# Experts' inner values split straight out of PSUM, size sums on ScalarE, conversion steps placed behind each scale, 4 KB rows for the second matrices

## The chip, the core and the metric

One core of a Trainium2 chip runs the whole program. Five engines take part: TensorE (PE in the rows; its weight loads are PEld), VectorE (DVE), ScalarE (ACT), GpSimd (POOL), and SyncE (SP), which issues nearly all the DMAs. Each engine works through its own list of instructions in order and waits on semaphores for the others. The metric is the device time of one execution in microseconds; lower is better.

## The reference

The program computes three layers one after the other: retention attention, a mixture of experts with a "sticky" choice of expert, and a Fourier mixing layer with a channel network. Only the middle one bears on the change:

```python
for b in range(B):
    for s in range(S):
        e = fresh_e if s == 0 or local_gate[b, s] < 0.5 else prev_e
        h = np.maximum(x[b, s] @ w1[e], 0.0)        # w1[e]: 512 x 1024
        out[b, s] = p[e] * (h @ w2[e])              # w2[e]: 1024 x 512
# last layer: ch = np.maximum(un @ w_ch1, 0.0) @ w_ch2, both matrices given as 64-bit floats
```

There are 2304 tokens and 8 experts. Everything is wanted at about fp32 accuracy.

## The kernel before

**Halves.** TensorE is fed fp16. Every fp32 operand is divided by a power-of-two scale and written as two fp16 tiles, high and low, and a product is the sum of three: high·high, low·high, high·low. For a weight matrix this is done on the chip, per piece of 128 rows x 1024 values (8 pieces per expert: 0 to 3 are the first matrix, 4 to 7 the second, which is loaded with two 2 KB rows per partition):

- `load` (L224): one 512 KB DMA from SP into a buffer of the pool `wst`.
- `absmax`/`size` (L234 on ScalarE by a sum of absolute values, L236 on VectorE by a maximum): the size of the piece. The table `SUMS` puts pieces 0 and 1 on VectorE and 2 to 7 on ScalarE.
- `peak` (L250, L251, L255): VectorE joins four sizes and writes a diagonal, `diag`; `spread` (L260 on TensorE, L261 on VectorE): a matmul of 128x128 with that diagonal brings the largest size to all partitions; `scale` (L266, L269): VectorE makes the scale `ws` and its inverse.
- `split`: `high` (L276, ScalarE, needs `ws`) and `low` (L281, VectorE, needs the high half).

**Conversion.** In the same stage VectorE converts the channel matrices of the last layer, which come as 64-bit floats, in 14 jobs of 128x1024 values: SP loads 1 MB (`conv.load`, L322, tile `raw`, two buffers), `first` is three instructions (L294, L296, L298), `second` two (L303, L306), `store` writes 512 KB (L338), `conv.absmax` takes the size (L234 or L236, alternately).

**An expert** has two steps. In the *hidden* step TensorE makes eight blocks f = 0..7 of the inner values (`products`, L807: 12 matmuls of n columns each, n = 416, 320, 320, 320, 288, 288, 128 for experts 1 to 7). Each block has a PSUM bank of the pool `p1`, which has four. `relu` takes a block away: ScalarE writes max(x, 0) as fp32 to a tile `r` (L818), ScalarE rounds that to the high half (L820), GpSimd subtracts the two for the low half (L822). In the *outputs* step the tokens go in tiles of 128: 24 matmuls per tile (L834, eight chunks of three), then a copy with the factor `fs` on ScalarE (L846) and an indirect DMA from GpSimd (L848). A rest of 64 or 32 tokens is done as 2 or 4 matmuls side by side.

**What sets the order.** The instructions are emitted by hand. `halves(weights, conv, n, slots)` gives the side jobs of step n (even: hidden of expert n/2, odd: its outputs), and the table `SLOTS` (one dictionary for even, one for odd steps) gives each a place between 0 and 8; all jobs that fall into one block or one tile are emitted, in the order of their places, ahead of that block's `relu` or that tile's copy. Step n splits the matrix that step n + 1 reads, sizes that of step n + 2 and loads that of step n + 3. In a hidden step TensorE does block 0, then the `spread` matmul of the expert's own second matrix, then blocks 1 to 7. In an outputs step the `spread` of the next expert's first matrix stands behind the fourth chunk of the first tile. Experts 0 and 1 start by hand (`begin`, `parts`, `first`, `convert`). On SP the token fetch for expert e + 1 (`fetch`, L1003: a transposing DMA, and L1016, L1019 for the indices) stands at the head of the hidden step of expert e. The last expert's rest is done by `Late` in the stage behind.

## Time and profile before

| what | us |
|---|---|
| median of three runs | 809.13 (806.35 to 814.45) |
| the profiled execution | 809.86 |
| its span in the trace | 808.1 |
| TensorE busy in the span | 741.5 (92%) |
| VectorE busy | 604.2 (75%) |
| ScalarE busy | 418.9 (52%) |
| GpSimd busy | 189.6 (23%) |

The page's table in 40 slices (20.2 us each) shows attention in slices 0 to 6, the experts in slices 6 to 17, and the last layer behind. All times below are from the start of the span. A row of a timeline reads: start, duration, engine, line, instruction, tile written <- tiles read, shape, count; in brackets the idle time ahead of it and what ended that.

### The profile page before, as it was taken

The page shows a single profiled execution, that of the slowest core. Times are in us where ns is not written, and L with a number is a line of the kernel's source. Part 1 is how long each engine was busy: PE and PEld are TensorE (multiplying, and loading weights), DVE is VectorE, ACT ScalarE, POOL GpSimd, SP SyncE. Part 2 cuts the span into 40 slices and gives each one's busy share as a digit, 9 for nine tenths or more (in the row PEclk, how much of TensorE's full clock was granted, in tenths as well). Part 3 has the DMA queues.
Part 4 walks back from the last instruction along what each step waited for, and adds up shares of the span by engine and source line. Part 5 has one row for each costly group of instructions (what it writes and reads, how often), then busy time and mean ns, then how long its engine had stood idle before and what let it go on. Part 6 is the DMA issues. An engine that isn't in the chain of part 4 may idle for free. (4 is left out here: it accounts for less than half of the span.)

```text
span 808.1 us, 17327 instructions
## 1 busy us (share of the span) xinstructions
PE 741.5 (92%) x6571; PEld 552.4 (68%) x6571; DVE 604.2 (75%) x1390; ACT 418.9 (52%) x857; POOL 189.6 (23%) x289
## 2 busy tenths in 40 slices
PE   8898898899899898789998999989889999999996
PEld 5687775546556555566644547868778888888885
DVE  3578988877898898857787986978958495737362
ACT  1356654778788787864744643515423361504140
POOL 3566442544355245322100002010010101010101
PEclk9999999999999999999998999999999999999998
DMA  9998349889899889932256357620380016110000
GB/s 294 348 302 312 108 131 306 226 296 374 312 280 322 319 248 310 351 110 91 84 175 236 127 192 204 188 68 2 112 198 2 27 53 171 53 33 21 27 2 27
DMA packets 91932, 142.30 MB, mean 176 GB/s; under 512 B 48116, under 2 KB 49017, under 8 KB 90814
## 3 DMA queue, kind: packets, MB, share of 16 engines
q1 hardware_dynamic: 87246, 126.78, 48.9%
q0 software_dynamic: 4592, 14.31, 4.6%
q8 instruction: 54, 0.88, 0.4%
q14 instruction: 40, 0.33, 0.1%
HBM read 97.55 MB, written 35.12 MB: 164 GB/s over the span
## 5 line engine op out<-in xcount | busy, mean ns | idle before, releaser
L1613 PE MATMUL g<-gxt,wh 128*128 128x256 f16 (+1 forms) x992 | 143.5, 285 | 3.6 <-DMA gxt<-un 3.4
L1927 PEld LDWEIGHTS <-hd 128*128 128x128 f16 x1176 | 114.7, 98 | 26.6 <-issue 6.4
L1613 PEld LDWEIGHTS <-wh 128*128 128x128 f16 x1056 | 103.1, 98 | 29.7 <-issue 8.4
L281 DVE SCALAR_TENSOR_TENSOR wl<-wst,ws,wh 128x1024 f16<-128x1024 f32 (+1 forms) x82 | 102.9, 1288 | 20.4 <-ACT wh L276 20.1
L1787 POOL DMA_INDIRECT out<-u,orow x18 | 19.1, 1064 | 391.2 <-DVE u L1956 293.3
L276 ACT ACTIVATE wh<-wst,ws 128x1024 f16<-128x1024 f32 x80 | 88.8, 1141 | 35.5 <-DVE ws L269 35.5
L807 PE MATMUL ps<-xt,wh 128*128 128x320 f16 (+4 forms) x544 | 81.3, 292 | 6.6 <-DMA xt<-xs 3.6
L807 PEld LDWEIGHTS <-wh 128*128 128x128 f16 x640 | 59.4, 103 | 38.7 <-issue 20.8
L834 PE MATMUL ps<-wh,hid 128*128 128x512 f16 (+2 forms) x528 | 84.2, 302 | 0.5 <-POOL hid L822 0.5
L1927 PE MATMUL g<-wh,hd 128*128 128x256 f16 x448 | 78.3, 273 | 2.9 <-DVE s L1898 1.6
L1613 PE MATMUL g<-gxt,wl 128*128 128x256 f16 (+1 forms) x496 | 80.5, 285 | 0.0
L1898 DVE SCALAR_TENSOR_TENSOR s<-g,r 128x256 f32<-128x256 f32 x168 | 53.1, 370 | 31.3 <-ACT hd L1892 30.5
L834 PEld LDWEIGHTS <-hid 128*128 128x128 f16 (+2 forms) x792 | 46.3, 100 | 42.5 <-issue 2.5
L822 POOL TENSOR_TENSOR hid<-r,hid 128x320 f16<-128x320 f32 (+3 forms) x64 | 64.0, 1011 | 41.4 <-ACT hid L820 40.8
L1956 DVE SCALAR_TENSOR_TENSOR u<-g,ffs,u 128x256 f32<-128x256 f32 (+1 forms) x63 | 34.1, 567 | 49.3 <-PE g L1927 48.7
L1891 ACT ACTIVATE r<-g 128x256 f32<-128x256 f32 x56 | 21.2, 379 | 92.8 <-PE g L1613 86.8
L1927 PE MATMUL g<-e,hd 128*128 128x256 f16 x504 | 61.2, 276 | 5.4 <-DVE u L1956 4.4
L1871 ACT ACTIVATE hd<-s 128x640 f16<-128x640 f32 x56 | 41.3, 737 | 46.8 <-DVE s L1898 46.8
L1927 PE MATMUL g<-wl,hd 128*128 128x256 f16 x224 | 61.1, 273 | 0.0
L1613 PEld LDWEIGHTS <-wl 128*128 128x128 f16 x528 | 51.8, 98 | 11.8 <-issue 1.1
L234 ACT ACTIVATE wh<-wst 128x1024 bf16<-128x1024 f32 x51 | 53.5, 1050 | 9.1 <-DMA wst<-in_moe_w 5.1
L834 PE MATMUL ps<-wl,hid 128*128 128x512 f16 (+2 forms) x264 | 56.3, 302 | 0.0
(303 smaller groups left out, 1352.3 us busy)
## 6 DMA issues: line engine op xcount, KB each, us to landing
wst<-in_moe_w SPq DMA_DIRECT2D x64, 512.0 KB
raw<-in_ch SPq DMA_DIRECT2D x14, 1024.0 KB
qk<-in_qkv SPq DMA_DIRECT2D x18, 512.0 KB
vk<-in_qkv SPq DMA_DIRECT2D x16, 512.0 KB
pair<-ch SPq DMA_DIRECT2D x32, 256.0 KB
ch<-d SPq DMA_DIRECT2D x14, 512.0 KB
...
```

Of the source, the lines that this page charges most:

```text
L234: self.nc.scalar.activation(out=x, in_=t, func=ACTF.Abs, accum_out=self.am[:, j : j + 1])
L276: self.nc.scalar.activation(out=self.dst[0][:, j, :], in_=self.pieces[j], func=ACTF.Copy, scale=self.by(j))
L281: self.nc.vector.scalar_tensor_tensor(out=l[:, j, c], in0=self.pieces[j][:, c], scalar=self.by(j), in1=h[:, j, c], op0=ALU.mult, op1=ALU.s ...
L807: nc.tensor.matmul(out=ps, lhsT=m[:, k, 128 * f : 128 * f + 128], rhs=xt[:, x + k, :], start=(k == 0 and i == 0), stop=(k == 3 and i == 2),)
L822: e.tensor_tensor(out=l[:, f, :], in0=r, in1=h[:, f, :], op=ALU.subtract)
L834: nc.tensor.matmul(out=ps[r * j : r * j + r, 0:d], lhsT=hid[x][:, f, 128 * t : 128 * t + r], rhs=m[:, 4 + f // 2, c : c + d], start=(f == ...
L1613: nc.tensor.matmul(out=ps, lhsT=m[:, k + 4 * (f // 8), 128 * (f % 8) : 128 * (f % 8) + 128], rhs=xt[x][:, k, :], start=(k == 0 and i == 0) ...
L1871: nc.scalar.activation(out=hd[:, 0, 2:7], in_=s, func=ACTF.Copy, scale=C2 / 2)
L1891: nc.scalar.activation(out=r, in_=p[:, 1:3], func=ACTF.Relu)
L1898: V.scalar_tensor_tensor(out=d, in0=x, scalar=0.0, in1=y, op0=ALU.max, op1=op)
L1927: nc.tensor.matmul(out=ps, lhsT=hid[k][:, y, x, :], rhs=E[w][m][k], start=(k == 0 and m == y == 0), stop=(k == 7 and y == 1),)
L1956: V.scalar_tensor_tensor(out=y, in0=p, scalar=fs[:, c : c + 1], in1=y, op0=ALU.mult, op1=ALU.add)
```

## The change

- **relu.** ScalarE writes the high half of a block directly from PSUM (one instruction in place of two), and VectorE makes the low half from the same PSUM bank: max(x, 0) - high, in place of GpSimd's subtraction. The factor `C1` goes into the scales (`W1_TOP`, `X_TOP`), so that no factor is applied on the way.
- **Sizes.** All sizes of weights and of conversion jobs are taken on ScalarE (`sums=S0` for all).
- **Order.** New `SLOTS`; conversion jobs run one step further ahead than before; in step 2 (hidden of expert 1) jobs 2 and 3 both stand at place 0. Loads of both matrices of expert e + 2 stand in the outputs step of expert e (the second ones at `ahead`), `fetch` stands behind the first splits, the factors of the outputs go among VectorE's side jobs (`factors`). Expert 2's pieces 4 to 7 are loaded in `sizes`.
- **Second matrix.** A partition gets two neighbouring rows (one run of 4 KB) in place of two rows 128 apart (2 x 2 KB). So that the inner values meet the right rows, the split of the first matrix reads every second column (`turned`), and `outputs` takes the chunks as 0, 4, 1, 5, 2, 6, 3, 7.

The diff, cut to its core:

```diff
+    def turned(self, j, c=slice(0, 1024)):
+        h, l, x = self.dst[0][:, j, c], self.dst[1][:, j, c], self.pieces[j]
+        if self.one or j > 3:
+            return h, l, x[:, c]
+        by = lambda w: w.rearrange("k (a q) -> k a q", q=512)
+        return by(h), by(l), x.rearrange("k (q a) -> k a q", a=2)[:, c.start // 512 : c.stop // 512, :]
...
     def high(self, j):
-        self.nc.scalar.activation(out=self.dst[0][:, j, :], in_=self.pieces[j], func=ACTF.Copy, scale=self.by(j))
+        h, _, x = self.turned(j)
+        self.nc.scalar.activation(out=h, in_=x, func=ACTF.Copy, scale=self.by(j))
...
-def relu(nc, e, ps, r, hid, f):
-    nc.scalar.activation(out=r, in_=ps, func=ACTF.Relu, scale=C1)
+def relu(nc, ps, hid, f, r=None):
     h, l = hid
-    nc.scalar.copy(out=h[:, f, :], in_=r)
+    if r is not None:
+        nc.scalar.activation(out=r, in_=ps, func=ACTF.Relu)
+        ps = r
+    nc.scalar.activation(out=h[:, f, :], in_=ps, func=ACTF.Relu)
     yield
-    e.tensor_tensor(out=l[:, f, :], in0=r, in1=h[:, f, :], op=ALU.subtract)
+    nc.vector.scalar_tensor_tensor(out=l[:, f, :], in0=ps, scalar=0.0, in1=h[:, f, :], op0=ALU.max, op1=ALU.subtract)
...
-    for f in range(8):
+    for s, f in enumerate((0, 4, 1, 5, 2, 6, 3, 7)):
...
 SLOTS = [
     dict(
-        split=(0, 0, 1, 2),
-        load=(1.5, 2.5, 2.5, 4.5),
-        size=(3.6, 4.6, 5.6, 5.7),
-        first=1.4,
+        own=-1,
+        second=0,
+        split=(0.1, 1.1, 2.1, 3.1),
+        raw=1.2,
+        store=1.3,
+        fetch=1.4,
+        size=(2.6, 3.6, 4.6, 5.6),
         peak=6.3,
-        bound=6.4,
     ),
     dict(
-        split=(0.5, 1.5, 2.5, 3.5),
+        own=-1,
+        first=(0, 4.2),
+        factors=0.2,
+        split=(0.5, 0.6, 1.5, 2.7),
+        second=2.8,
         load=(2, 3, 4, 5),
         size=(3.1, 4.1, 4.6, 5.2),
-        rest=0.2,
-        early=0.25,
-        first=0.3,
-        second=3.6,
-        store=6.9,
-        raw=0.5,
-        other=2.0,
-        bound=5.9,
+        raw=5.5,
+        store=5.6,
         peak=7.3,
+        ahead=(7.4, 7.5, 7.6, 7.7),
     ),
 ]
...
+    if n == 2:
+        at(S["second"], conv.first, 2)
+        ends(2)
+        at(S["peak"], conv.absmax, 2)
+        at(S["second"], conv.first, 3)
+    if n % 2 and n + 1 < DONE:
+        at(S["first"][0], conv.first, n + 1)
+    ends(n + 1)
+    if n % 2 and n + 2 < DONE:
+        at(S["first"][1], conv.first, n + 2)
...
-            r = wk.tile([128, CAP], FP32, tag="r", name="r", bufs=3)[:, 0:n]
-            for _ in relu(nc, nc.gpsimd, ps, r, hid, f):
+            for _ in relu(nc, ps, hid, f):
                 pass
...
-                    A["moe_w2"][e, 256 * j : 256 * j + 256, :].rearrange("o (a p) d -> p (o a) d", p=128)
+                    A["moe_w2"][e, 256 * j : 256 * j + 256, :].rearrange("o (p a) d -> (o p) a d", a=2).rearrange("p a d -> p (a d)")
```

`ends(j)` places `second`, `store` and the load of job j + 2.

**VectorE in the hidden step of expert 1**, from the scale of the expert's second matrix on (`wl` is a weight's low half, `d` and `raw` a conversion job, `am` a size, `hid` the low half of a block of inner values). Before:

```order
L269 RECIPROCAL ws<-wi 128x1
L281 SCALAR_TENSOR_TENSOR wl_78<-wst,ws,wh_77 128x1024 x3
L294 TENSOR_SCALAR d<-raw 128x1024
L296 TENSOR_SCALAR d<-d 128x1024
L298 TENSOR_SCALAR d<-d 128x1024
L281 SCALAR_TENSOR_TENSOR wl_78<-wst,ws,wh_77 128x1024
L236 TENSOR_REDUCE am<-wst 128x1 x2
```

And now, up to the low half of block 1:

```order
L302 TENSOR_SCALAR d<-raw 128x1024
L304 TENSOR_SCALAR d<-d 128x1024
L306 TENSOR_SCALAR d<-d 128x1024
L311 SCALAR_TENSOR_TENSOR d<-raw,d 128x1024
L314 SCALAR_TENSOR_TENSOR d<-raw,d 128x1024
L302 TENSOR_SCALAR d<-raw 128x1024
L304 TENSOR_SCALAR d<-d 128x1024
L306 TENSOR_SCALAR d<-d 128x1024
L311 SCALAR_TENSOR_TENSOR d<-raw,d 128x1024
L314 SCALAR_TENSOR_TENSOR d<-raw,d 128x1024
L291 SCALAR_TENSOR_TENSOR wl_78<-wst,ws,wh_77 128x1024
L833 SCALAR_TENSOR_TENSOR hid<-ps_2360,hid 128x416
```

Two whole conversion jobs, 2 and 3, have moved ahead of the first low halves, and the low half of block 0 of the inner values stands behind all of them.

**TensorE at the start of block 4 of expert 1** with the semaphores that are waited for (`ps_2458` and `ps_2454` are block 3, `ps_2477` and `ps_2472` block 4, the fifth block, which takes the bank of block 0 again). Before:

```order
L807 MATMUL ps_2458<-xt,wh_77 128x416
L807 LDWEIGHTS wh_77
L807 MATMUL ps_2477<-xt,wh_77 128x416 [waits Activation_49]
L807 LDWEIGHTS wh_77
L807 MATMUL ps_2477<-xt,wh_77 128x416
```

And now:

```order
L815 MATMUL ps_2454<-xt,wh_77 128x416
L815 LDWEIGHTS wh_77
L815 MATMUL ps_2472<-xt,wh_77 128x416 [waits DVE_49]
L815 LDWEIGHTS wh_77
L815 MATMUL ps_2472<-xt,wh_77 128x416
```

The bank was given back by ScalarE and is now given back by VectorE.

**VectorE in the outputs step of expert 2**, from the middle of the step (`wg`, the answer to the spread matmul) to the next diagonal. Before:

```order
L261 TENSOR_REDUCE wg<-ps_3057 128x1
...
L303 SCALAR_TENSOR_TENSOR d<-raw,d 128x1024
L306 SCALAR_TENSOR_TENSOR d<-raw,d 128x1024
L294 TENSOR_SCALAR d<-raw 128x1024
L296 TENSOR_SCALAR d<-d 128x1024
L298 TENSOR_SCALAR d<-d 128x1024
L281 SCALAR_TENSOR_TENSOR wl_78<-wst,ws,wh_77 128x1024 x4
L303 SCALAR_TENSOR_TENSOR d<-raw,d 128x1024
L306 SCALAR_TENSOR_TENSOR d<-raw,d 128x1024
...
L255 TENSOR_SCALAR diag<-idn,wm 128x128
```

And now:

```order
L302 TENSOR_SCALAR d<-raw 128x1024
L304 TENSOR_SCALAR d<-d 128x1024
L306 TENSOR_SCALAR d<-d 128x1024
L1069 TENSOR_TENSOR fs<-wi 128x1
L1070 TENSOR_SCALAR fs<-mt,fs 128x3
L1164 TENSOR_SCALAR mt<-mt,side_1982 128x1
L291 SCALAR_TENSOR_TENSOR wl_78<-wst,ws,wh_77 128x1024 x4
L311 SCALAR_TENSOR_TENSOR d<-raw,d 128x1024
L314 SCALAR_TENSOR_TENSOR d<-raw,d 128x1024
L302 TENSOR_SCALAR d<-raw 128x1024
L304 TENSOR_SCALAR d<-d 128x1024
L306 TENSOR_SCALAR d<-d 128x1024
```

One `second` has left the stretch (it stands in the hidden step, right behind the scale there), one `first` and the three small instructions for the factors have come in. The diagonal follows the last row.

## Rows read from the trace of the kernel before

**Rows 1.** The page, part 2: busy tenths of TensorE in 40 slices

```profile
PE   8898898899899898789998999989889999999996
```

**Rows 2.** Who TensorE waited for: us in total, times, longest

```profile
PE peak L260 <- DVE diag L255: 11.4, 6, 2.5
```

**Rows 3.** Five windows between spread matmuls of experts 2 to 7: engines' busy us

```profile
sum 145.42, PE 129.50 PEld 80.74 DVE 132.35 ACT 118.14 POOL 63.36; mean PE 25.90 PEld 16.15 DVE 26.47 ACT 23.63 POOL 12.67
```

**Rows 4.** Timeline of TensorE in the period from 218.94 to 248.27

```profile
218.94 0.22 PE L260 MATMUL peak<-diag,onesb 128*128 128x128 bf16 x1 [1.88 <-DVE diag L255]
...
230.40 0.59 PE L834 MATMUL ps<-wh,hid 128*128 128x512 f16 x2
...
233.91 0.23 PE L260 MATMUL ps<-diag,onesb 128*128 128x128 bf16 x1 [0.76 <-DVE diag L255]
```

**Rows 5.** Timeline of VectorE in the outputs step of expert 2

```profile
205.58 0.14 DVE L1043 SCALAR_TENSOR_TENSOR fs<-wi 128x1 f32<-128x1 f32 x1
...
206.02 0.28 DVE L261 TENSOR_REDUCE wg<-ps 128x1 f32<-128x128 f32 x1
...
206.61 1.20 DVE L303 SCALAR_TENSOR_TENSOR d<-raw,d 128x1024 int32<-128x1024 int32 x1
...
208.99 0.69 DVE L294 TENSOR_SCALAR d<-raw 128x1024 int32<-128x1024 int32 x1
...
211.05 4.87 DVE L281 SCALAR_TENSOR_TENSOR wl<-wst,ws,wh 128x1024 f16<-128x1024 f32 x4
...
218.60 0.29 DVE L255 TENSOR_SCALAR diag<-idn,wm 128x128 bf16<-128x128 f32 x1
```

**Rows 6.** Timelines of VectorE, and of GpSimd, in the hidden step of expert 3

```profile
221.15 1.29 DVE L281 SCALAR_TENSOR_TENSOR wl<-wst,ws,wh 128x1024 f16<-128x1024 f32 x1 [1.28 <-ACT wh L276]
228.41 1.81 DVE L281 SCALAR_TENSOR_TENSOR wl<-wst,ws,wh 128x1024 f16<-128x1024 f32 x1
226.77 4.10 POOL L822 TENSOR_TENSOR hid<-r,hid 128x320 f16<-128x320 f32 x3 [0.76 <-ACT hid L820]
```

**Rows 7.** Groups of instructions: count, busy us, mean ns, idle before

```profile
L236 DVE TENSOR_REDUCE am<-wst 128x1 f32<-128x1024 f32 x12 | 14.0, 1204 | 0.0
L234 ACT ACTIVATE wh<-wst 128x1024 bf16<-128x1024 f32 x40 | 41.9, 1048 | 5.3 <-DMA wst<-in_moe_w 5.1
L820 ACT CAST hid<-r 128x320 f16<-128x320 f32 x24 | 11.0, 458 | 0.8
L1898 DVE SCALAR_TENSOR_TENSOR s<-g,r 128x256 f32<-128x256 f32 x168 | 53.1, 370 | 31.3 <-ACT hd L1892 30.5
L544 DVE SCALAR_TENSOR_TENSOR xr<-tr,mx,xr 128x512 f16<-128x512 f32 x18 | 13.4, 747 | 7.3 <-ACT xr L542 7.3
L276 ACT ACTIVATE wh<-wst,ws 128x1024 f16<-128x1024 f32 x57 | 63.3, 1141 | 35.2 <-DVE ws L269 35.2
```

**Rows 8.** Timelines of VectorE, SyncE and TensorE around the hidden step of expert 1

```profile
167.25 0.92 DVE L294 TENSOR_SCALAR d<-raw 128x1024 int32<-128x1024 int32 x1 [4.28 <-DMA raw<-in_ch]
178.32 0.69 DVE L294 TENSOR_SCALAR d<-raw 128x1024 int32<-128x1024 int32 x1
156.44 0.54 SPq L322 DMA_DIRECT2D raw<-in_ch  x1
160.78 0.51 SPq L322 DMA_DIRECT2D raw<-in_ch  x1
156.42 0.86 PE L807 MATMUL ps<-xt,wh 128*128 128x416 f16 x4
171.19 0.59 PE L834 MATMUL ps<-wh,hid 128*128 128x512 f16 x2
```

**Rows 9.** One window behind a wait: PE busy, ..., then granted clock, DMA, GB/s

```profile
335.20:338.60 3.40, 3.06 (x30) 3.06 (x30) 1.70 (x5) 1.98 (x2) 0.66 (x2) 0.50 1.03 418
```

**Rows 10.** Timeline of TensorE: expert 7's second spread, and the stage behind

```profile
335.54 0.27 PE L260 MATMUL peak<-diag,onesb 128*128 128x128 bf16 x1 [2.51 <-DVE diag L255]
...
347.73 0.44 PE L807 MATMUL ps<-xt,wh 128*128 128x160 f16 x4
```

More of the change, by code (lines that the diff above doesn't have):

```diff
@@ L54 @@
 NROWS = 12
-C1 = 2.0**-13
+W1_TOP = 2.0**-7
+X_TOP = 2.0**-6
 C2 = 2.0**-18
@@ L266, in scale @@
         nc.vector.tensor_scalar(
-            out=inv, in0=g, scalar1=2.0**-13, scalar2=2.0**-100, op0=ALU.mult, op1=ALU.max
+            out=inv, in0=g, scalar1=W1_TOP if i == 0 and not self.one else 2.0**-13, scalar2=2.0**-100, op0=ALU.mult, op1=ALU.max
         )
@@ L866, in __init__, with hidden @@
         self.n, self.hid = CAPS[E - 1] - HEAD, None
-    def hidden(self, fs, bank, room):
+    def hidden(self, fs, bank):
         n = self.n
@@ L939, in halves, with ends @@
             at(S["size"][p], w.absmax, 4 * i + p)
-    w, i = matrix(n + 3)
-    if w and not (w.one and i):
-        for p in range(4):
-            at(S["load"][p], w.load, 4 * i + p)
-    if n < DONE:
-        at(S["first"], conv.first, n)
-    if n % 2 and n < DONE:
-        at(S["rest"], conv.second, n - 1)
-        at(S["early"], conv.store, n - 1)
-        if n + 1 < DONE:
-            at(S["raw"], conv.load, n + 1)
-        at(S["second"], conv.second, n)
-        at(S["store"], conv.store, n)
-        if n + 2 < DONE:
-            at(S["other"], conv.load, n + 2)
-        at(S["bound"], conv.absmax, n - 1)
-    if n % 2 == 0 and 1 < n <= DONE:
-        at(S["bound"], conv.absmax, n - 1)
+    if n % 2:
+        for m, k in ((n + 3, "load"), (n + 4, "ahead")):
+            w, i = matrix(m)
+            if w and not (w.one and i):
+                for p in range(4):
+                    at(S[k][p], w.load, 4 * i + p)
+    for k, f in others:
+        at(S[k], *f)
+    def ends(j):
+        if j < DONE:
+            at(S["second"], conv.second, j)
+            at(S["store"], conv.store, j)
+            if j + 2 < DONE:
+                at(S["raw"], conv.load, j + 2)
+    if n == 2:
+        at(S["second"], conv.first, 2)
[7 more added lines that the diff above has]
+        at(S["first"][1], conv.first, n + 2)
     w, i = matrix(n + 2)
@@ L1094, in sizes @@
         conv.absmax(0)
-    fs = factors(weights(0), mt0, 2)
+        for p in range(4, 8):
+            weights(2).load(p)
+    fs, fill = factors(weights(0), mt0, 2)
+    fill()
     for t in range(2):
@@ L1112, in moe @@
         xt, mt = X.pop(e)
-        if e > 0 and e + 1 < E:
-            fetch(e + 1)
         tiles = (n + 127) // 128
-        todo = halves(weights, conv, 2 * e, 8) if e else first
+        todo = halves(weights, conv, 2 * e, 8, [("fetch", (fetch, e + 1))] if e + 1 < E else ()) if e else first
         hid = wk.tile([128, 2, 8, n], FP16, tag="hid", name="hid", padded_shape=[128, 2, 8, CAP])
@@ L1126, in moe, with sides @@
                 pad(e + 2)
-            r = wk.tile([128, CAP], FP32, tag="r", name="r", bufs=3)[:, 0:n]
-            for _ in relu(nc, nc.gpsimd, ps, r, hid, f):
+            for _ in relu(nc, ps, hid, f):
                 pass
-        fs = factors(w, mt, tiles + (end.n + 127) // 128 if e == E - 1 else tiles)
+        fs, fill = factors(w, mt, tiles + (end.n + 127) // 128 if e == E - 1 else tiles)
         if e == E - 1:
             end.fs = fs
-        for i, m in ((n // 128, n % 128), (tiles + end.n // 128, end.n % 128 if e == E - 1 else 0)):
-            if m:
-                to, k = mt[:, i, 0:1], 128 // m
-                nc.vector.tensor_scalar(out=to, in0=to, scalar1=float(k), scalar2=side[k], op0=ALU.mult, op1=ALU.add)
+        def sides(mt=mt, tiles=tiles, n=n, e=e):
+            for i, m in ((n // 128, n % 128), (tiles + end.n // 128, end.n % 128 if e == E - 1 else 0)):
+                if m:
+                    to, k = mt[:, i, 0:1], 128 // m
+                    nc.vector.tensor_scalar(out=to, in0=to, scalar1=float(k), scalar2=side[k], op0=ALU.mult, op1=ALU.add)
+        late = 0 < e < E - 1
+        if not late:
+            fill()
+            sides()
         if e == E - 1:
@@ L1140, in moe @@
             yield
-        todo = halves(weights, conv, 2 * e + 1, tiles) if e else [[sizes]]
+        todo = halves(weights, conv, 2 * e + 1, tiles, [("factors", (f,)) for f in (fill, sides) if late]) if e else [[sizes]]
         for t in range(tiles):
@@ L1145, in moe @@
             out(w, hid, mt, fs, t, n, todo[t], amid)
-    end.hidden(range(LATE), bank, lambda: wk.tile([128, CAP], FP32, tag="r", name="r", bufs=3))
+    end.hidden(range(LATE), bank)
     ctx.close()
@@ L1563, in bank @@
         return q.tile([128, 512], FP32, tag=tag, name="bank")
-    late.hidden(range(LATE, 8), bank, lambda: wk.tile([128, 512], FP32, tag="gr", name="r"))
+    late.hidden(range(LATE, 8), bank)
     tr.root()
```

47 lines of the change are left out of this document (23 added, 24 removed).

## The prediction, made blind

> **What bounds the kernel now.** I began with the page's table of slices: the experts fill slices 6 to 17, and TensorE is not quite full there [rows 1]. The change touches hardly anything else, so everything below is about those slices. The waits of TensorE come next: the largest one that an edited instruction can move is that of the `spread` matmul for VectorE's diagonal, 11.4 us in 6 waits [rows 2]. Then I cut the steady part into five periods, each from the spread of a second matrix to that of the next one (experts 2 to 7). Together they last 145.42 us, in which TensorE is busy for 129.50, VectorE for 132.35 (91%) and ScalarE for 118.14 [rows 3]. A timeline of one period shows where TensorE's slack lies: 1.88 us ahead of the first spread, 0.76 ahead of the second, both for `diag`, and nothing else [rows 4]; 248.27 - 218.94 = 29.33, less 2.64, is 26.69. The same timeline gives the step lengths: seven blocks of inner values take 230.40 - 218.94 = 11.46, or 1.63 each. VectorE's rows behind `wg` run without a gap from 206.02 to 218.60 + 0.29 = 218.89 [rows 5]. So the chain of VectorE, from one spread to the next diagonal, sets the pace of this stage, with TensorE 10% below it. A gain must shorten that chain, and whatever makes it longer costs time.
>
> **The change part by part.**
>
> *Inner values.* ScalarE loses one cast of 0.46 per block. VectorE gains one instruction per block that reads PSUM, which the trace lacks. Its neighbours are 0.370 for 256 columns and 0.747 for 512, both 1.45 ns per column [rows 7], so 320 columns cost 0.47, 416 cost 0.60 and 128 about 0.2. I take 0.48, with 0.37 and 0.75 as ends. Eight per expert are 3.8 us of new work on the engine that sets the pace. From SBUF VectorE takes 4.87 / 4096 = 1.19 ns per column [rows 5], so the PSUM bank is the dearer source by a fifth. [...] GpSimd's subtractions go, and VectorE runs beside them slowly now: a low half took 1.81 at 228.41, while GpSimd subtracted, and 1.29 at 221.15 [rows 6]. That and two shorter rows of the same kind give back about 1.5 per expert.
>
> *Sizes.* VectorE loses 12 weight sizes of 1.204 and seven of conversion jobs, which ScalarE does in 1.05 [rows 7]: about 3.5 us per expert leave VectorE. ScalarE gets as much as its eight casts (3.7) free, and stays behind VectorE's pace.
>
> *Hidden step, 320 columns, from the spread.* The scale is ready after 0.94 (221.15 - 1.28 - 218.94). VectorE idles there for 1.28, waiting for ScalarE's high half [rows 6]; now `second`, 2.38 (206.61 to 208.99, [rows 5]), stands there and covers it. A low half (1.2) and the first `hid` (0.48) follow, so the bank of block 0 is free at 0.94 + 2.38 + 1.2 + 0.48 = 5.0. TensorE has then just done blocks 1 to 3 (0.22 + 3 x 1.63 = 5.1): no wait, though only just. The next three blocks need 1.2 + 0.48 = 1.68 of VectorE against 1.63, so the step ends at about 11.7 (11.46 before).
>
> *Outputs step.* The spread in the middle of the first tile comes 233.91 - 0.76 - 230.40 = 2.75 into the step, and without its wait `wg` starts 0.26 later. From `wg` to the end of `diag` VectorE took 12.87. It loses `second` (2.38), gains `first` (208.99 to 211.05, 2.06) and the factors (205.58 to 206.02, 0.44) [rows 5], and keeps the four low halves: 13.0. So the diagonal is ready 2.75 + 0.26 + 13.0 = 16.05 into the step, against 248.27 - 230.40 = 17.87 before. Period: 11.7 + 16.05 = 27.75 for experts 2 to 4. For 5, with 288 columns, I take 27.45. Expert 6 has no conversion left in its outputs; ScalarE's highs and sizes set about 13.6 there, so 25.0. The sum is 3 x 27.75 + 27.45 + 25.0 = 135.7 in place of 145.4: **-9.7**.
>
> *The hidden step of expert 1.* Conversions 2 and 3 now stand whole ahead of the first low half, and the first `hid` stands behind that. The queue of SyncE reads the same up to the load of `raw`(3), so both loads are issued when they are now, 156.44 and 160.78. The first lands at 167.25: VectorE waits 4.28 for it [rows 8]. That costs nothing now, because ScalarE gives the banks back. In the changed kernel it does: `hid` of block 0 is queued behind the waiting instruction, TensorE's fifth block waits for that bank, and the outputs wait for the block. Conversion 2 ends at about 171.85. `raw`(3) lands between 160.78 + 10.81 = 171.6 (the delay of `raw`(2)) and 178.3, where VectorE takes it without a wait; I take 173.3, nearer the low end, because the queue ahead of it is no longer. Then conversion 3 (2.06 + 2.38) ends at 177.9, the low half and `hid` at 179.7. Before, seven blocks ran from 156.42 to 171.19, 2.11 each, so the fifth began at 162.75. Loss: 179.7 - 162.75 = **16.9**, with 15.3 and 21.8 as ends. [...] Together **+18.6**. Conversions 0 and 1 delay `hid` 4 and 7 of expert 0 by some 5 us in the same way, but that lies ahead of the loads, and the stall swallows it.
>
> *Expert 7, 128 columns.* Each of its first four blocks now waits for a low half and a `hid` on VectorE, some 1.5, against 0.65 on TensorE. From the spread: 0.94 + 1.28 + 1.5 = 3.7 for block 4, then three times 1.45, a block (0.65) and the outputs (5.3) make 14.1, against 347.73 - 335.54 = 12.19 [rows 10]: **+1.9**.
>
> *At nothing.* The rows of 4 KB move the same bytes. The loads start earlier, but VectorE and not DMA ends the waits above. The order of the chunks, the scales and the moved fetches change no duration; what hides them is TensorE's slack of 1 us per period, and if one showed it would cost that much per period.
>
> **Sum.** +18.6 - 9.7 + 1.9 = +10.8 on an execution of 809.86, which lies 0.73 above the median of 809.13: 820.7, as a median **820.0**.
>
> **The rivals.** (A) The above: one stall at expert 1 outweighs a gain in each period. Chance 0.55, 814 to 826.
>
> (B) The gain is greater: without GpSimd's interference and with the casts gone, VectorE's chain drops below TensorE's, and the periods come down to TensorE's own 129.50 [rows 3], a gain of 15.9. Then +18.6 - 15.9 + 1.9 = +4.6: 813.7, no change that can be measured. For it: only 0.8 to 1.2 us per period separate the two in my sum. Against it: 13.0 from `wg` to `diag` is made of rows without gaps, and would have to be 12.0. Chance 0.22.
>
> (C) The strided reading of the first matrix (every second value) slows ScalarE's high half, for which no row exists: between 0 and twice its 1.141 [rows 7]. Doubled, four per expert add 4.6 to ScalarE's 23.6 per period [rows 3], 28.2, and the gain is gone: 829. VectorE reads every second word of `raw` at 208.99 in the 0.69 of its contiguous neighbours [rows 5], which speaks against it. Chance 0.08. [...]
>
> (D) The other side: `raw`(2) and `raw`(3) land before 159, since fewer bytes are in the way. VectorE's burst is then only 2 x 4.44, block 4 starts at 157.3 + 8.9 + 1.2 + 0.6 + ScalarE's delay, about 170, +7.5, and with -9.7 and +1.9 the time is 809, no slower. It decides from a landing of the first at 159 in place of 167; the same queue on SyncE speaks against it [rows 8]. Chance 0.15, with a third of it below 801 if B comes too.
>
> **How the numbers follow.** About 1% (8 us) is what a measurement of this kernel can tell from no change, so slower begins at 817.2 and faster ends at 801.0. A lies above 817.2 except for its low end (0.08), C does: slower 0.47 + 0.08 = 0.55. B, two thirds of D and A's low end are the same: 0.22 + 0.10 + 0.08 = 0.40. Faster is the rest of D, 0.05. The range leaves out C, the best of D and the worst of A: 808 to 828; A's own is 814 to 826.
>
> **What would show it.** Right: one wait of TensorE for VectorE's `hid` (L833) of some 17 us near 163 to 180, with VectorE waiting there for `raw`; L833 near 0.47 for 320 columns; periods of 27 to 28 with the wait for `diag` near 1 us; L302 to L306 at 0.69 each throughout. Wrong: `raw`(2) landing well before 167; a gap of TensorE at block 4 of each later expert (the 5.0 against 5.1 fell the other way, and A becomes dearer); L276 above 1.2 for the first matrices; periods below 26.5.

## The result, and the profile after

| | before | changed |
|---|---|---|
| median, us (17 runs each, on the same chips) | 811.72 (806.35 to 814.89) | 818.40 (814.61 to 821.46) |
| ratio | | 1.0072, 95% interval 1.0052 to 1.0093 |
| the profiled execution, us | 809.86 | 816.25 |
| its span | 808.1 | 814.5 |

The changed kernel is 0.7% slower: inside the range, 1.6 us from the forecast of 820.0, and within the 1% that counts as no change here. By that 1% the outcome is "the same", to which the forecast gave 0.40, against 0.55 for "slower". The change itself is +6.7 us by the medians, where +10.8 was forecast. So the case is not whether it moved, but what the sum is made of. The page's slices of the changed kernel, to be held against [rows 1]:

```profile
PE   7898898729999998979998999989899999999996
```

Slice 8 (163 to 183 us) falls to 2, and the slices behind it are fuller than before. TensorE's waits (total, times, longest) say the same, against [rows 2]:

```profile
PE ps L815 <- DVE hid L833: 18.4, 7, 14.7
PE peak L260 <- DVE diag L255: 6.1, 5, 2.3
...
PE ps L845 <- DVE hid L833: 3.2, 1, 3.2
```

The wait for the diagonal went from 11.4 to 6.1, and a new one came, 14.7 us long in one piece. The stall in time order, first VectorE, then SyncE's two loads, then TensorE:

```profile
160.62 0.16 DVE L269 RECIPROCAL ws<-wi 128x1 f32<-128x1 f32 x1
168.68 0.69 DVE L302 TENSOR_SCALAR d<-raw 128x1024 int32<-128x1024 int32 x1 [7.89 <-DMA raw<-in_ch]
...
174.72 0.69 DVE L302 TENSOR_SCALAR d<-raw 128x1024 int32<-128x1024 int32 x1 [1.37 <-DMA raw<-in_ch]
...
179.31 1.28 DVE L291 SCALAR_TENSOR_TENSOR wl<-wst,ws,wh 128x1024 f16<-128x1024 f32 x1
180.50 0.58 DVE L833 SCALAR_TENSOR_TENSOR hid<-ps,hid 128x416 f16<-128x416 f32 x1
```

```profile
158.39 0.43 SPq L330 DMA_DIRECT2D raw<-in_ch  x1
...
162.69 0.43 SPq L330 DMA_DIRECT2D raw<-in_ch  x1
```

```profile
165.53 0.87 PE L815 MATMUL ps<-xt,wh 128*128 128x416 f16 x4
181.14 1.55 PE L815 MATMUL ps<-xt,wh 128*128 128x416 f16 x4 [14.74 <-DVE hid L833]
```

VectorE has the scale of the second matrix at 160.8 and then does nothing for 7.89 us, because conversion 2 stands first in its queue. The `hid` that frees TensorE's bank (the low half of block 0) starts at 180.50, and block 4 starts 0.6 later. The windows of the changed kernel from spread to spread (PE, PEld, DVE, ACT, POOL busy, then granted clock, DMA share, GB/s), and the first 4.8 us behind the stall:

```profile
159.85:210.68 50.83, 36.09 (x268) 18.54 (x267) 31.89 (x49) 26.12 (x41) 4.53 (x9) 0.83 0.87 300
210.68:238.12 27.44, 26.54 (x196) 16.66 (x194) 24.34 (x41) 23.68 (x41) 4.02 (x7) 1.00 0.93 289
...
320.06:344.82 24.76, 23.58 (x242) 14.98 (x242) 17.93 (x33) 21.91 (x37) 1.85 (x4) 1.00 0.90 291
sum 134.14, PE 127.42 PEld 80.38 DVE 115.02 ACT 115.61 POOL 17.40; mean PE 25.48 PEld 16.08 DVE 23.00 ACT 23.12 POOL 3.48
```

```profile
181.10:185.90 4.80, 4.76 (x14) 2.08 (x14) 4.80 (x6) 0.41 (x1) 0.00 (x0) 0.50 0.92 311
```

With that the 6.4 us between the two spans are accounted for, each stage from one spread matmul (`peak`) to the next:

| stage | before | changed | difference | forecast |
|---|---|---|---|---|
| up to the first spread | 136.85 | 138.47 | +1.6 | 0 |
| expert 0 (to 156.37, 159.85) | 19.52 | 21.38 | +1.9 | 0 |
| expert 1 (to 190.12, 210.68) | 33.75 | 50.83 | +17.1 | +18.6 |
| five periods, experts 2 to 6 | 145.42 | 134.14 | -11.3 | -9.7 |
| expert 7 (to 347.73, 357.79) | 12.19 | 12.97 | +0.8 | +1.9 |
| the stage behind | 460.4 | 456.7 | -3.7 | 0 |

The first and the last line can't be put down to the change: in all the profiled runs of this document, whatever they change, the first spread lies between 136.4 and 140.3 and the stage behind lasts 456.7 to 461.5. The four lines between them, which the forecast was about, add up to +8.5, where the forecast has +10.8.

### The profile page after: what moved, and what is told of

It reads as the page before. It is cut to its first block, busy times and chain, and to the rows that moved or that the text cites. A ratio compares the mean times of both kernels' runs of the same rounds, so it can differ in the third digit from the quotient of the medians.

```text
span 814.5 us, 17226 instructions
## 1 busy us (share of the span) xinstructions
PE 739.8 (91%) x6571; PEld 549.4 (67%) x6571; DVE 592.8 (73%) x1432; ACT 414.5 (51%) x829; POOL 126.0 (15%) x225
## 5 line engine op out<-in xcount | busy, mean ns | idle before, releaser
L1645 PEld LDWEIGHTS <-wh 128*128 128x128 f16 x1056 | 103.0, 98 | 27.4 <-issue 6.0
L291 DVE SCALAR_TENSOR_TENSOR wl<-wst,ws,wh 128x1024 f16<-128x1024 f32 (+1 forms) x82 | 100.7, 1253 | 9.9 <-ACT wh L286 9.7
L286 ACT ACTIVATE wh<-wst,ws 128x1024 f16<-128x1024 f32 x80 | 92.3, 1178 | 28.6 <-DVE ws L269 26.8
L815 PEld LDWEIGHTS <-wh 128*128 128x128 f16 x640 | 57.3, 99 | 52.2 <-issue 34.7
L234 ACT ACTIVATE wh<-wst 128x1024 bf16<-128x1024 f32 x66 | 69.3, 1053 | 4.3 <-DVE wst L314 4.3
L1988 DVE SCALAR_TENSOR_TENSOR u<-g,ffs,u 128x256 f32<-128x256 f32 (+1 forms) x63 | 34.1, 568 | 49.3 <-PE g L1959 48.7
L859 POOL DMA_INDIRECT x<-y,mt x25 | 28.3, 1132 | 217.0 <-ACT y L857 190.3
L1645 PEld LDWEIGHTS <-wl 128*128 128x128 f16 x528 | 51.9, 98 | 11.7 <-issue 1.1
```

The source lines that it names most:

```text
L234: self.nc.scalar.activation(out=x, in_=t, func=ACTF.Abs, accum_out=self.am[:, j : j + 1])
L286: self.nc.scalar.activation(out=h, in_=x, func=ACTF.Copy, scale=self.by(j))
L291: self.nc.vector.scalar_tensor_tensor(out=l, in0=x, scalar=self.by(j), in1=h, op0=ALU.mult, op1=ALU.subtract)
L815: nc.tensor.matmul(out=ps, lhsT=m[:, k, 128 * f : 128 * f + 128], rhs=xt[:, x + k, :], start=(k == 0 and i == 0), stop=(k == 3 and i == 2),)
L859: nc.gpsimd.indirect_dma_start(out=x2[:, :].rearrange("t (k d) -> (t k) d", k=k), out_offset=bass.IndirectOffsetOnAxis(ap=mt, axis=0), in_ ...
L1645: nc.tensor.matmul(out=ps, lhsT=m[:, k + 4 * (f // 8), 128 * (f % 8) : 128 * (f % 8) + 128], rhs=xt[x][:, k, :], start=(k == 0 and i == 0) ...
```

## The experiments

Times are medians. Each ratio is to the kernel before, run on the same chip. The last two columns are us of the profiled execution: expert 1 from its spread to that of expert 2 (33.75 before), and the five periods (145.42 before).

| run | us | ratio (95%) | expert 1 | five periods |
|---|---|---|---|---|
| changed kernel | 818.4 | 1.0072 (1.0052 to 1.0093) | 50.8 | 134.1 |
| x1_conv_behind | 817.9 | 1.0069 (1.0040 to 1.0098) | 47.4 | 136.4 |
| x2_gpsimd_lows | 822.6 | 1.0130 (1.0070 to 1.0189) | 46.0 | 143.5 |
| x5_rows_2k | 818.5 | 1.0054 (1.0019 to 1.0089) | 50.9 | 134.6 |
| x6_before_sizes | 814.7 | 1.0027 (0.9991 to 1.0063) | 35.5 | 145.7 |
| x7_fetch_behind | 807.0 | 0.9922 (0.9885 to 0.9959) | 38.0 | 134.1 |
| x8_not_ahead | 802.8 | 0.9864 (0.9807 to 0.9920) | 33.6 | 135.2 |
| x9_sizes_vector | 832.2 | 1.0231 (1.0177 to 1.0284) | 49.3 | 149.9 |
| x10_not_ahead_e0 | 801.4 | 0.9878 (0.9814 to 0.9941) | 33.6 | 135.2 |
| x11_order_alone | 806.0 | 0.9917 (0.9890 to 0.9943) | 35.7 | 136.1 |
| x12_first_in_hidden | 803.9 | 0.9886 (0.9846 to 0.9926) | 34.4 | 138.9 |
| x13_raw_later | 806.2 | 0.9926 (0.9898 to 0.9955) | 33.8 | 139.3 |
| x14_store_early | 806.2 | 0.9923 (0.9894 to 0.9952) | 33.8 | 138.9 |

### Where the stall comes from

**x1: the two conversions behind the low halves.**

```diff
     if n == 2:
-        at(S["second"], conv.first, 2)
+        S = dict(S, second=5.1, store=5.2, raw=5.3)
+        at(5.1, conv.first, 2)
         ends(2)
-        at(S["peak"], conv.absmax, 2)
-        at(S["second"], conv.first, 3)
+        S = dict(S, second=7.1, store=7.2, raw=7.3)
+        at(7.1, conv.first, 3)
```

(The size of conversion 2 goes to the head of the next step.)

> The changed kernel, except that in the hidden step of expert 1 conversion 2 stands ahead of block 5's low half and conversion 3 ahead of block 7's, with their stores and loads behind them (in the changed kernel both stand ahead of the first low half). Theory (one stall: the low half of block 0 queues behind VectorE's waits for the two raw tiles): TensorE's wait of 14.7 us at block 4 of expert 1 goes, and with it the 2.0 us at half clock behind it; a wait of under 1 us for the last low half is left at the end of the first outputs tile. Time 818.4 - 16 = about 802, about 1.2% below the kernel before. Rival (the loads are late whatever the order, and the work they hold up only stalls somewhere else): the wait for raw moves into the step, the outputs of expert 1 wait for low halves, and no more than 5 us are won: 813 or more.

The time hardly moved: the number expected missed by 16 us, and the rival's came out. The wait at block 4 is gone, as the theory says, but the step is only 3.5 us shorter. Its timelines of SyncE and VectorE:

```profile
170.22 10.06 SPq L1030 DMA_TRANSPOSE xt<-xs  x1
...
184.96 1.36 SPq L330 DMA_DIRECT2D raw<-in_ch  x1
```

```profile
194.59 0.69 DVE L302 TENSOR_SCALAR d<-raw 128x1024 int32<-128x1024 int32 x1 [12.12 <-DMA raw<-in_ch]
```

Behind the conversions stood their SyncE part too: the load of `raw`(4) now came behind the token fetch, which held SyncE for 10.06 us, and VectorE's next conversion, at the head of the outputs step, waited 12.12 us for it. TensorE paid for that, and for the last low half, in three smaller waits (3.4 for the diagonal, 3.3 for a bank, 2.5 for the low half); the mean granted clock was 0.75 from 180 to 185 us, behind the wait of 2.5, and 0.74 from 200 to 207, behind that of 3.3. What was left open: is it the order on SyncE, or are the DMA queues full?

**x7: the fetch moved behind those loads as well.**

```diff
-    S = SLOTS[n % 2]
+    S = dict(SLOTS[n % 2], fetch=7.9 if n == 2 else 1.4)   # on top of x1
```

> The kernel with conversions 2 and 3 behind blocks 4 and 6 of expert 1 (x1_conv_behind), and the token fetch for expert 2 also moved, on SyncE, behind the loads of raw 4 and 5 (place 7.9 in place of 1.4 of that step). There SyncE spent 10.1 us on the transposing fetch, issued raw 4 at 185.0, and VectorE waited 12.1 us for it ahead of the splits. Theory (the second stall is that wait, made by the order on SyncE): raw 4 is issued at about 175.5 and lands by 184; VectorE's wait falls below 3 us, and of the stalls of expert 1 only the 2.5 for the last low half with its half clock (4 us together) stays. The spread of expert 2's second matrix comes at 198 to 200 in place of 207.1; time 808 to 811. Rival (the DMA queues are full there, a load issued earlier lands no earlier): the wait stays above 8 us, time 815 or more.

```profile
174.53 0.91 SPq L330 DMA_DIRECT2D raw<-in_ch  x1
```

```profile
183.23 0.69 DVE L302 TENSOR_SCALAR d<-raw 128x1024 int32<-128x1024 int32 x1 [1.88 <-DMA raw<-in_ch]
```

`raw`(4) is issued at 174.5 and used at 183.2; VectorE waits 1.88 in place of 12.12, and expert 1 takes 38.0, a little less than expected. From issue to use the load takes about as long as in x1 (8.7 us against 9.6). So it was the order on SyncE. The two moves together take 12.9 of the stall's 17.1, and the kernel is 0.8% faster than before.

**x8: no catching-up at all.**

```diff
     if n == 2:
-        at(S["second"], conv.first, 2) ... conv.first, 3
+        S = dict(S, second=5.1, store=5.2, raw=5.3)        # fetch=5.4 here
+        at(5.1, conv.first, 2)
-    if n % 2 and n + 1 < DONE: at(S["first"][0], conv.first, n + 1)
-    ends(n + 1)
-    if n % 2 and n + 2 < DONE: at(S["first"][1], conv.first, n + 2)
+    if n % 2 and n < DONE: at(S["first"][0], conv.first, n)
+    ends(n)
+    if n % 2 and n + 1 < DONE: at(S["first"][1], conv.first, n + 1)
```

(and `absmax` one step later likewise)

> The changed kernel without the catching-up at expert 1: its hidden step does conversion 2 alone (ahead of block 5's low half, with the fetch behind the load of raw 4), and from there each step does the jobs that the changed kernel does one step earlier; relu, sizes, places and 4 KB rows stay. VectorE then has 4.4 us less to do by the end of expert 1's hidden step, and the last conversion falls into expert 6's outputs again. Theory (the whole loss is the catching-up, the gain of the periods is not tied to it): no stall of more than 2 us at expert 1, so 156.4 to 190.1 of the kernel before (33.8 us) is 34 to 35 here and not 50.8; the five periods gain 11.3 less 2 for expert 6. Time 803 to 806, about 1% below the kernel before. Rival (the periods are short only because VectorE runs a step ahead): they come out at 29 again, and the time at 811 or more.

```profile
158.33:191.94 33.61, 33.61 (x267) 17.82 (x266) 27.37 (x44) 25.08 (x39) 4.44 (x9) 1.00 0.99 336
```

TensorE is busy through all 33.61 us of expert 1: the stall is gone, all of it, and the periods keep their 27.44 (only that of expert 6, which gets its conversion back, goes from 24.76 to 25.87). 802.8 is 1.4% below the kernel before; 803 to 806 was expected.

**x10: and the old way of halving in expert 0 alone.**

```diff
+            if e == 0:   # ScalarE: r = max(ps, 0), h = round(r); GpSimd: l = r - h
+                old = wk.tile([128, CAP], FP32, tag="r", name="r", bufs=3)[:, 0:n], nc.gpsimd
+            for _ in relu(nc, ps, hid, f, *old):
```

> x8_not_ahead with, in expert 0 alone, the old way of halving the inner values (ScalarE writes fp32 and rounds, GpSimd subtracts), so that the last low halves of expert 0 don't queue behind conversions 0 and 1 on VectorE. In the changed kernel the outputs of expert 0 waited 3.2 us for them, and the spread of expert 1 came 3.5 us later than before. Theory: the wait goes and 1.5 to 3 us are won: 801 to 804. Rival (expert 1 waits for the diagonal or its tokens anyway): within 1 us of x8_not_ahead.

The outputs of expert 0 no longer wait for VectorE's low halves (0.6 for GpSimd's, against 1.7 in x8 and 3.2 in the changed kernel), and the spread of expert 1 comes 19.80 after that of expert 0, against 20.89 in x8. 801.4 against 802.8 is inside the spread of four runs; the trace shows 1.1 us, which is less than the 1.5 to 3 expected and hardly more than the rival allows.

### What makes the periods shorter

**x2: the low halves back on GpSimd** (the old `relu`, as in the diff of x10, for every expert; all else as changed).

> The changed kernel with one part undone: in the experts' loop ScalarE again writes max(x, 0) as fp32 and rounds it, and GpSimd subtracts; the order, the sizes on ScalarE and the 4 KB rows stay. Theory: ScalarE gives the banks back again, so block 4 of expert 1 no longer waits for the low half of block 0; but the low half of the first piece of the second matrix still stands behind both conversions (done at about 180.6), and the outputs of expert 1, which would begin at about 171 to 174, wait for it: the stall of 16.7 shrinks to 7 to 9 and moves to the outputs. In the periods behind, VectorE loses 3.8 us of low halves but ScalarE has 23.6 + 3.5 + 0.5 = 27.6 us of work per period, so it becomes the bound: periods of 27.5 to 28.5 in place of 27.45. Time 810 to 816. Rival 1 (the bank's release has nothing to do with the stall): the wait at block 4 stays at 14 to 15 us, 818 to 822. Rival 2 (the low halves on VectorE are what keeps the periods long): periods fall to TensorE's 26.5 or less, and the time to 806 or less.

TensorE in expert 1, and one period:

```profile
182.88 0.58 PE L851 MATMUL ps<-wl,hid 128*128 128x512 f16 x1 [9.09 <-DVE wl L291]
```

```profile
233.69:263.07 29.38, 27.12 (x194) 16.48 (x194) 22.49 (x33) 27.11 (x47) 10.22 (x15) 1.00 0.95 307
```

The first half of the expectation came out: nothing waits at block 4, and the outputs wait 9.09 us (7 to 9 expected) for the weight's low half, which stands behind the same two conversions. The bank is what passed VectorE's wait on to TensorE in the hidden step. The second half was too kind: the periods are 29.4, not 27.5 to 28.5, and the time is 822.6, not 810 to 816. ScalarE is busy 27.11 of 29.38 us; its casts of the last blocks queue behind the sizes, GpSimd gets them late, and TensorE's outputs wait for those halves (0.48 and 0.40 in this period).

**x6: the sizes on ScalarE, in the kernel before.**

```diff
-                made[i] = Weights(..., sums=SUMS if i else S0)
+                made[i] = Weights(..., sums=S0)      # c1 and c2 likewise
```

> The kernel before with one part of the change alone: all sizes of weights and of conversion jobs on ScalarE. VectorE loses 12 x 1.20 and 7 x 1.20 us; ScalarE gains 19 x 1.05 and keeps its casts, 23.6 + 3.5 = 27.1 us per period. Theory (VectorE's chain sets the period, and a size is part of it only where it stands between wg and diag): the periods of 29.1 lose the 2.4 us of the two weight sizes in the step or the 1.2 of a conversion size, but ScalarE at 27 comes close: periods 27.5 to 28.5, time 811.7 - 3 to - 8, no new stall at expert 1. Rival 1 (ScalarE becomes the bound at once): periods 29 or longer, 811 to 815. Rival 2 (the sizes were the whole gain): periods at 27.4 as in the changed kernel.

```profile
222.37:251.94 29.57, 27.11 (x196) 16.34 (x194) 23.34 (x33) 26.71 (x47) 13.35 (x15) 1.00 0.92 304
```

This is rival 1: VectorE falls from 26.7 to 23.3 us in this period and nothing is won (1.0027, 0.9991 to 1.0063). ScalarE, with 26.7, takes its place.

**x9: the sizes back on VectorE, in the changed kernel** (the reverse of the diff above).

> The changed kernel with one part undone: pieces 0 and 1 of each expert matrix set and every second conversion job are sized on VectorE again. Theory (the gain of a period needs both the sizes on ScalarE and the low halves straight from PSUM; each alone leaves one of the two engines with 27 us): VectorE's two sizes of 1.2 stand between blocks 2 and 3 of the hidden step, where it has no slack, so the step and the period grow by 2.0 to 2.4, to 29.5 or so; the stall at expert 1 stays at 14 to 17. Time 826 to 831. Rival (VectorE has 3.8 us of slack in a period, so the sizes fit): periods within 0.5 of 27.4, time within 3 of 818.4.

```profile
237.74:268.29 30.55, 26.86 (x195) 16.63 (x194) 27.48 (x44) 20.53 (x33) 3.87 (x7) 1.00 0.93 300
```

```profile
247.02 0.70 PE L816 MATMUL ps<-xt,wh 128*128 128x320 f16 x4 [0.89 <-DVE hid L834]
...
249.74 0.43 PE L816 MATMUL ps<-xt,wh 128*128 128x320 f16 x2 [0.93 <-DVE hid L834]
```

```profile
254.42 1.21 DVE L237 TENSOR_REDUCE am<-d 128x1 f32<-128x1024 f32 x1
```

30.55 per period and 832.2: both weight sizes stand between low halves for which TensorE's banks wait (1.8 us in this period). The time is just above the 826 to 831 expected, and the period is 1 us above the 29.5. The expectation left out the size of the conversion job, the last row above: it stands right behind `wg`, in the stretch that leads to the diagonal, and TensorE's wait for `diag` is 1.9 us in this period where it was 0.9.

**x11: the order alone**, both others undone (x10 with x2's `relu` everywhere and x9's sizes).

> x10_not_ahead_e0 with relu and sizes both undone in all experts: ScalarE rounds, GpSimd subtracts, VectorE sizes pieces 0 and 1 and every second conversion job, as in the kernel before; what is left of the change is the new order (second behind the scale of the hidden step, first in the outputs, the loads earlier) and the 4 KB rows. So far one of the two undone alone gave periods of 29.4 (low halves on GpSimd) and 30.5 (sizes on VectorE), both in place 27.4. Theory (the order is what shortens the period, and the other two edits only hold each other up): VectorE's hidden step is 0.9 + 2.4 + 4 x 1.3 + 2.4 + 1.5 for GpSimd's company = 12.4, plus 1.2 for the conversion size, done before the spread in the outputs at 14.5; ScalarE has 23.6. Then the outputs run as in the changed kernel and the period is 27.3 to 27.9, the time 801 to 805. Rival (the low halves straight from PSUM and the sizes on ScalarE are the gain): periods of 29 or more, time 810 or more.

```profile
220.87:248.82 27.95, 26.69 (x194) 16.58 (x194) 25.83 (x37) 23.92 (x41) 11.28 (x15) 1.00 0.98 326
...
sum 136.05, PE 127.55 PEld 79.92 DVE 125.09 ACT 118.62 POOL 53.90; mean PE 25.51 PEld 15.98 DVE 25.02 ACT 23.72 POOL 10.78
```

27.95 and 806.0 us are just above the 27.9 and 805 that were expected at most, and far from the rival's 29 and 810. This shows where most of the gain comes from. With the new order, a period of 320 columns takes (in us, the second of the three such periods)

| | sizes on ScalarE | sizes partly on VectorE |
|---|---|---|
| low halves on VectorE, from PSUM | 27.44 | 30.55 (x9) |
| low halves on GpSimd | 29.38 (x2) | 27.95 (x11) |

In x11 the conversions run a step later than in the three others; x8 shows that this by itself leaves the period at 27.44. The order takes 9.4 of the 11.3 us off the five periods (145.42 to 136.05). The two other edits, together, take about 1 more (136.05 to 135.17, x11 against x10), and the last 1 us (135.17 to 134.14) is the period of expert 6, which has no conversion left when they run a step earlier. Undoing only one of the two edits costs the changed kernel 9.4 (x2) or 15.7 us (x9) of its periods. The intervals of x11 and x10 overlap, so the difference between 806.0 and 801.4 is not shown; by the traces about 2 us of it lie in expert 1 and 1 in the periods. The moves that make up the order were not tried one by one.

**x5: rows of 2 KB, no stride, chunks 0 to 7.**

```diff
-                    ....rearrange("o (p a) d -> (o p) a d", a=2).rearrange("p a d -> p (a d)")
+                    ....rearrange("o (a p) d -> p (o a) d", p=128)
-        if self.one or j > 3:
+        if True:
```

> The changed kernel with one part undone: the second matrices come in two rows of 2 KB per partition again, the first matrices are read without a stride, and the chunks are taken in the order 0 to 7. Theory: neither DMA nor ScalarE's high halves end a wait of TensorE in the periods, so the time stays within 1.5 us of 818.4; ScalarE's high half of the first matrices falls from at most 1.27 us to 1.14. Rival (the strided reading or the longer packets matter): 3 us or more either way, in the periods between the spread matmuls of experts 2 to 7 or in the landing of raw at expert 1.

818.5 and 134.61 us: no difference in time. ScalarE's high halves, in x5 and in the changed kernel:

```profile
L286 ACT ACTIVATE wh<-wst,ws 128x1024 f16<-128x1024 f32 x80 | 89.4, 1141 | 28.5 <-DVE ws L269 25.5 <-DVE fs L1069 2.0 <-DVE wg L261 1.0
```

```profile
L286 ACT ACTIVATE wh<-wst,ws 128x1024 f16<-128x1024 f32 x80 | 92.3, 1178 | 28.6 <-DVE ws L269 26.8 <-DVE fs L1069 1.8
```

### Can the last microsecond per period be had

**x12: one more conversion step in the hidden step** (on x10).

```diff
+    elif n % 2:
+        S = dict(S, second=0, raw=1.9, store=1.95)
     ends(n)
+    if n % 2 == 0 and 2 < n and n + 1 < DONE:
+        at(5.1, conv.first, n + 1)
```

> x10_not_ahead_e0 with one more conversion step moved: from expert 2 on, first of the job that the outputs need stands in the hidden step, ahead of block 5's low half, where VectorE has only 0.48 us of work for each 1.63 of TensorE, and in the outputs second stands at the head in its place. VectorE's stretch from wg to the diagonal loses 2.06 us (13.3 to 11.2). Theory (that stretch still sets the period, by the 0.9 to 2.3 us that TensorE waits for the diagonal): the waits for the diagonal in experts 2 to 6 fall below 0.3, the periods to TensorE's own 26.5, 5 to 6 us in all: 795 to 798, 2% below the kernel before. Rival (the low halves of blocks 5 to 7 come 2 us later and the outputs wait for them, or raw is not there yet): as much is lost as is won, 800 to 803.

```profile
192.96:219.34 26.38, 26.38 (x197) 16.66 (x194) 24.12 (x41) 23.66 (x41) 3.33 (x6) 1.00 0.95 315
219.34:247.57 28.23, 26.87 (x197) 16.56 (x195) 24.33 (x41) 23.10 (x39) 3.48 (x6) 1.00 0.96 315
```

```profile
284.10 1.06 ACT L234 ACTIVATE wh<-wst 128x1024 bf16<-128x1024 f32 x1 [4.43 <-DMA wst<-in_moe_w]
```

The first period is TensorE's own, 26.38, without a wait. In the next ones ScalarE waits for a piece to size, up to 4.43 us, and the halves of a block stand behind that. The sum is 138.9 and nothing is won, for a reason that neither the theory nor the rival of x12 had. **x13** puts the load and the store back behind the pieces (`raw=5.5, store=5.6`), **x14** the load alone (`store=1.9`):

> x12_first_in_hidden with the load and the store of a conversion job on SyncE back behind the loads of the weight pieces in the outputs (places 5.5 and 5.6 in place of 1.9 and 1.95). In x12 the period of expert 2 was 26.4, TensorE's own, but ScalarE then waited 2.2 to 4.4 us for a piece to size in the hidden steps of experts 3 and 5, and the halves of block 2 queued behind that. Theory (1 MB of raw ahead of those pieces made them late): these waits go, the periods are 26.4 to 26.8 for experts 2 to 4, 25 to 26 for 5 and 6; sum 130 to 132 in place of 135.2 (x10) and 138.9 (x12), time 796 to 800. Rival (the pieces are late because DMA is full, whatever the order): ScalarE still waits over 1 us per period, 801 to 804.

> x13_raw_later with the store of a conversion job alone (512 KB) early in the outputs, place 1.9, and the load of raw (1 MB) behind the weight pieces, place 5.5. In x13 the wait for a piece to size was gone, but first in the hidden step waited 1.6 to 3.4 us for the store that frees its tile, and the low halves behind it made the outputs wait 1 to 3 us. Theory (each wait is one transfer standing behind others on SyncE, and half the bytes ahead of the pieces are little enough): both waits below 0.5 us, the periods of experts 2 to 4 at 26.4 to 26.8, sum 130 to 132, time 796 to 800. Rival (no place for these transfers is free of a wait: the queues are full, DMA share 0.93 to 0.98): 801 to 806, with the wait on one of the two again.

VectorE's `first` of the hidden step of expert 3 in x13, and in x14:

```profile
233.02 0.69 DVE L302 TENSOR_SCALAR d<-raw 128x1024 int32<-128x1024 int32 x1 [2.77 <-DMA ch<-d]
```

```profile
233.29 0.69 DVE L302 TENSOR_SCALAR d<-raw 128x1024 int32<-128x1024 int32 x1 [1.73 <-DMA raw<-in_ch]
```

The wait went from the pieces to the store that frees the tile (neither the theory nor the rival of x13 had that), and from there to the load of `raw`, as the rival of x14 has it. The sums are 138.9 to 139.3 against x10's 135.2, and all three missed the 795 to 800 expected. Which of x8, x10 and x12 is the fastest their intervals don't tell. The DMA share is 0.92 to 0.98 in these periods, and in each of the three placings that were tried one kind of transfer is late. Whether less traffic would free it was not tried.

## Why the prediction was right, point by point

- **The number** is in part luck. The forecast added +10.8 to a median of 809.13 that came from three runs; the 17 runs beside the changed kernel's put the kernel before at 811.72. With that median it would have said 822.5, which is 4.1 from the 818.4 measured. The terms are off by less, +8.5 for +10.8, and the rest, -2.1, lies in the first and the last line of the table.
- **The stall of expert 1** was the term that decides the sign, and its mechanism came as written: VectorE waits for `raw`, `hid` of block 0 is queued behind it, TensorE's fifth block waits for the bank. `raw`(3) took 12.0 us from its issue to its use (162.69 to 174.72), 12.5 were taken. Block 4 began at 181.14; 179.7 was forecast, and the first spread already lies 1.6 later than before. The wait itself is 14.74 where 16.9 was the forecast, since the whole expert began 3.5 us later and the loads only 1.9 (158.39 against 156.44 [rows 8]), which leaves less to wait for. Above the 16.9 the forecast's 18.6 holds 1.7 for half clock behind the wait, half of the 3.40 us at a granted clock of 0.50 in [rows 9]. No run shows this 1.7; behind the wait of 14.74 the granted clock was 0.50 for 4.80 us, an estimated 2.4 lost. Sum 17.1 for 18.6.
- **The delay of expert 0** (+1.9 in the table) "lies ahead of the loads, and the stall swallows it", says the forecast. That held: counted from the first spread the loads are issued within 0.4 us of before, the delay shortens the stall by about as much as it costs, and experts 0 and 1 together take 19.0 us more for the 18.6 forecast. In x8, which has no stall to swallow it, the delay counts, and x10 gets 1.1 us of it back.
- **The periods** came out by their terms. Hidden step 11.48 (222.16 - 210.68; forecast 11.7), from there to the diagonal's spread 15.96 (16.05). TensorE at both ends of the outputs step, and VectorE from `wg` to the end of `diag`:

```profile
222.16 0.59 PE L845 MATMUL ps<-wh,hid 128*128 128x512 f16 x2
...
238.12 0.22 PE L260 MATMUL peak<-diag,onesb 128*128 128x128 bf16 x1 [0.91 <-DVE diag L255]
```

```profile
225.01 0.29 DVE L261 TENSOR_REDUCE wg<-ps 128x1 f32<-128x128 f32 x1 [1.04 <-PE ps L260]
...
228.12 4.86 DVE L291 SCALAR_TENSOR_TENSOR wl<-wst,ws,wh 128x1024 f16<-128x1024 f32 x4
...
237.79 0.29 DVE L255 TENSOR_SCALAR diag<-idn,wm 128x128 bf16<-128x128 f32 x1
```

  13.07 us, forecast 13.0; TensorE still waits 0.9 there, forecast 1. Expert 5: 27.04 for 27.45; expert 6: 24.76 for 25.0. The gain is 11.3 for 9.7. Where it lies shows in `wg`. The stretch behind it has not become shorter (12.87 before), but `wg` now starts 2.85 into the outputs step (222.16 to 225.01). Before, it started 4.95 into it (230.40 [rows 4] to 235.35), because the spread waited 0.76 for its diagonal [rows 4] and VectorE was then still at work on a conversion's size and the factors:

```profile
233.78 1.21 DVE L236 TENSOR_REDUCE am<-d 128x1 f32<-128x1024 f32 x1
...
235.35 0.28 DVE L261 TENSOR_REDUCE wg<-ps 128x1 f32<-128x128 f32 x1
```

  With the order alone (x11) it starts 3.2 into the step and waits there for TensorE:

```profile
235.52 0.29 DVE L262 TENSOR_REDUCE wg<-ps 128x1 f32<-128x128 f32 x1 [1.49 <-PE ps L261]
```

  So what the order does is to have VectorE done with its other work by the time the spread comes, and most of the gain is that; the forecast's sum has it (2.75 + 0.26), but does not say that the order alone is enough for it. Of relu and sizes the forecast priced each engine's loss and gain but not that either needs the other; x2, x9 and x11 show that.
- **The low half from PSUM** (mean ns in the changed kernel, from the groups of instructions):

```profile
L833 DVE SCALAR_TENSOR_TENSOR hid<-ps,hid 128x320 f16<-128x320 f32 x24 | 11.4, 487 | 3.7 <-ACT hid L831 3.7
...
L833 DVE SCALAR_TENSOR_TENSOR hid<-ps,hid 128x416 f16<-128x416 f32 x8 | 4.6, 587 | 4.2 <-ACT hid L831 4.2
...
L833 DVE SCALAR_TENSOR_TENSOR hid<-ps,hid 128x128 f16<-128x128 f32 x16 | 4.1, 283 | 0.1
```

  0.487, 0.587 and 0.283 for 0.48, 0.60 and 0.2. A price in proportion to the columns was wrong at 128: these three rows are close to 0.147 us and 1.06 ns per column.
- **Expert 7**: +0.8 for +1.9. TensorE at blocks 4 and 7 (both wait for a bank), at its outputs behind block 7, and at the stage behind:

```profile
348.57 0.38 PE L815 MATMUL ps<-xt,wh 128*128 128x128 f16 x4 [0.96 <-DVE hid L833]
...
352.75 0.38 PE L815 MATMUL ps<-xt,wh 128*128 128x128 f16 x4 [0.56 <-DVE hid L833]
...
353.42 0.38 PE L845 MATMUL ps<-wh,hid 128*128 128x512 f16 x1
...
357.79 0.44 PE L815 MATMUL ps<-xt,wh 128*128 128x160 f16 x4
```

  The blocks in series came as forecast: block 4 begins 3.75 behind the spread (3.7) and the next three follow at 1.39 each (1.45). The mis-sized term is the outputs behind them, 5.3: TensorE did four of their 24 matmuls between those blocks, in time that it would have waited, and 4.37 was left (353.42 to 357.79).
- **The rivals.** B (TensorE's own pace): the gain would have been 15.9, it is 11.3; x12's first period shows what that pace is, 26.38. C (strided reading): the strided high halves went up by 8%, not by 100%, and x5 shows it to cost nothing. One sign that the forecast named for being wrong did come with it, a high half above 1.2 for the first matrices (1.20 to 1.27). D: `raw`(2) landed at 168.7, not at 159.
